# A fused attention and gMLP kernel on one core: the scheduler's landing times of loads and transposes are padded, its transfer durations replaced, and all due times drawn anew

## The chip, the core and the metric

The kernel runs on one core of one Trainium2 chip. The metric is the device time of one launch in microseconds (us), the median of several runs of the same program. In the core, TensorE (PE) multiplies matrices and takes its stationary operand through a weight load (PEld). VectorE (DVE), ScalarE (ACT) and GpSimd (POOL) work on rows of up to 128 partitions, and SyncE (SP) issues all the kernel's transfers (DMAs). Each engine executes its own instruction list strictly in order and waits on semaphores for the others. SBUF is the on-chip memory, PSUM the small memory into which PE writes.

## The reference

Inputs are q, k, v of shape (4, 8, 1152, 64), which is 4 batches of 8 heads, and the weights of a gated MLP. Everything is float32.

```
q_pool = q.reshape(B, H, S // 2, 2, D).mean(axis=3)          # 576 pooled rows per head
scores = (q_pool @ k.T) / sqrt(D)                            # 576 x 1152
attn   = exp(scores - max) / (sum + 1e-9)
x      = (attn @ v), heads side by side                      # (4, 576, 512)

h    = gelu(x @ w_in)                                        # 512 -> 1024
u, v = h[..., :512], h[..., 512:]
v    = layernorm(v) * g_ln
v_s  = w_sg @ v + b_sg                                       # mixes the 576 positions
out  = x + (u * v_s) @ w_out
```

## The kernel before

**Units of work.** The 32 heads are taken as 16 pairs p (four pairs make a batch). In a pair, each head's 1152 keys are nine blocks j of 128 keys. A unit (`attend`, `main`, `unit_of`) is one block of one head against 512 pooled query rows. The last 64 query rows of a head are gathered into two tail units. A unit has two score matmuls (L463), the exponential on ACT (L471), a split of the result into two float16 halves (ACT L477, then a subtraction L482 on DVE or POOL), and twelve small matmuls that weigh the values into the accumulator `avp` (L491). Pairs 0 and 2 skip the split and weigh in float32 (L498).

**Preparing a pair** (`load`, `prepare`, `maxima`, `values`). SP loads k (tile `kr`, L239), q (`qr` and `qe`, L242 and L245) and v (`vr`, L249, or `va` directly, L253, for pairs 0 and 2). There is one buffer of each raw tile, so a pair's k can only be loaded when the pair before it has finished with `kr`. ACT sums the squares of k (L285), PE spreads the sum over the partitions (one small matmul, L288), and DVE makes a scale from it (L270 to L295). ACT and DVE then write k in two float16 halves (L318, L321), and SP transposes them (L325). The same is done for q (POOL L313 and L315, ACT L331, DVE L335, transposed at L339) and for v (L285, L288, L361, L364). PE then computes all the scores once only for their row maxima (L388), and DVE reduces them (L394, collected at L418). POOL splits the maxima (L424 to L426), and a third transpose (L429) puts them beside q so that the second score matmul subtracts them.

**The gMLP of a batch** (`project`, `gmlp`) comes after its 8 heads. PE transposes x (L565) and multiplies by w_in (L641). The layer norm has its statistics on DVE (L666), its normalisation on DVE (L680 writes a float32 row block, L684 its float16 half) and the other half on POOL (L688). Then PE mixes the positions (L641 with `wsg`, L741) and multiplies by w_out (L641 with `wout_h` and `wout_l`, twelve matmuls per output block). The matmuls of one batch's gMLP are spread among the attention units of the next. Only the last batch's stand alone at the end. The weights themselves are split into two parts early in the kernel (`weights`, with L857, L858, L864, L867 on DVE and L870, L876 on POOL).

**Order.** Nothing is issued in the order of the program text. Every piece of work is added to a list with its engine, an assumed duration, what it reads and writes, and a due time. `Schedule.run` then plays the list against a simple model of the engines while the program is built. Each engine takes, of its pieces that could start earliest, the one with the smallest due time. What comes out is only the order on each engine's list. On the chip the semaphores decide when anything starts. For a transfer the model says:

```
dma = max(t + 1.35, dma) + dur        # the queue is busy for dur
free[e] = max(t + issue, dma - AHEAD) # when SP can issue again
end = dma + 0.9                       # when the data count as landed
```

The due times come from tables of numbers (`D_LK` for the load of k, `D_X` for the maxima, and so on, with a column each for pairs 0, 1, 2, 3, 4 to 11, and 12 to 15), read by `lead`.

At the start PE also runs up to 40 matmuls on constant data (L804) that produce nothing the kernel needs.

Of the kernel before, what the change touches and what calls it, by code (L numbers as in the profile page):

```python
# [21 lines left out]
class Schedule:  # L22
# [11 lines left out]

    def add(self, eng, dur, fn, r=(), w=(), due=0.0, acq=None, rel=(), tab=None, start=0.0, port=False, issue=0.5):
        n = len(self.ops)
        deps = set()
        for t in r:
            if t in self.writer:
                deps.add(self.writer[t])  # L40
            self.readers.setdefault(t, []).append(n)
        for t in w:
            if t in self.writer:
                deps.add(self.writer[t])
            deps.update(self.readers.get(t, ()))
# [3 lines left out]
        self.ops.append((eng, dur, fn, deps, round(due + 0.00137, 2), acq, rel, tab, start, port, issue))  # L49

# [4 lines left out]
    def run(self, look):  # L55
        ops = self.ops
# [15 lines left out]
        for _ in ops:  # L72
            for e in engines:
# [3 lines left out]
                for i in can[e]:  # L77
# [3 lines left out]
                    if ops[i][9]:  # L81
                        t = max(t, port)
# [6 lines left out]
            t, i, e = min((t, i, e) for e, (t, i) in choice.items())  # L89
            _, dur, fn, _, _, acq, rel, tb, _, shared, issue = ops[i]  # L90
            can[e].remove(i)
# [38 lines left out]
def attention_gmlp_kernel(  # L130
# [102 lines left out]
    def load(p):  # L233
# [68 lines left out]
    def prepare(p):  # L302
# [5 lines left out]
        for h in range(2):  # L308
# [38 lines left out]
            add("SP", 0.41, k_copy, r=[f"k1{c}{h}"], w=[f"k2{c}{h}"], due=t + lead("KC", p) + h * HS[p > 0])  # L347
            add("DVE", 0.46, q_lo, port=True, r=[f"qs{h}", sct, f"n1{h}"], w=[f"n2q{h}"], due=t + lead("QL", p) + h * HS[p > 0])
# [21 lines left out]
    def maxima(p):  # L370
# [34 lines left out]
        for r in range(9):  # L405
# [6 lines left out]
            if r in (4, 8):  # L412
# [19 lines left out]
                add("POOL", 0.76, split, r=[], w=[f"nm{h}", f"n2m{h}"], due=due - 0.5)  # L432
                add("SP", 0.9, turn, issue=1.25, r=[f"n2q{h}", f"n2m{h}"], w=[f"q2{c}{h}"], due=due - 1)

# [394 lines left out]
    def weights(i):  # L829
# [47 lines left out]

        add("SP", 1.46 * ks, ld, r=["sgdone"], w=rt, due=due - 4)
        add("DVE", 0.68 * ks, s0, port=True, r=rt + ["sgdone"], w=mt + et, due=due)
# [133 lines left out]
KEEP = (0.5, 0.5)  # L1013
D_LK = (-1505.8, -1000.85, -165.08, 526.48, 736.52, 688.03)
D_LQ = (484.61, -1082.79, 1016.76, 1252.2, 668.71, 1.89)
D_LV = (281.6, 307.72, -557.03, 495.8, -509.12, -447.84)
D_SC = (165.08, -128.04, -685.32, -1035.46, -362.92, -1153.53)
D_PL = (-1835.97, -262.1, -273.75, 852.48, 106.54, -40.22)
D_QH = (-1892.34, 165.59, 721.49, 179.72, 662.34, 655.56)
D_KH = (138.62, 145.13, -178.82, -35.67, 780.77, 749.18)  # L1020
D_KC = (-142.4, 635.61, 29.25, -1173.71, -539.16, -997.0)
D_QL = (771.92, -299.43, -364.25, -671.26, 1125.27, 1471.97)
D_VS = (-861.69, -1728.92, 766.42, -696.66, -828.5, -432.59)
D_VH = (-464.47, 768.08, -814.46, -1485.68, 329.36, 378.93)
# [56 lines left out]
```

## Time and profile before

| what | value |
|---|---|
| runs | 680.47, 678.55, 679.84 us (median 679.84) |
| the profiled execution, its own time | 682.78 us |
| its span, first to last instruction | 681.0 us |
| PE busy | 638.4 us (94% of the span) |
| DVE, ACT, POOL busy | 527.8, 523.4, 396.9 us |
| weight loads (PEld) busy | 459.0 us, beside PE |
| mean share of the 16 DMA engines | 43.0% for the kernel's own queue |

The profile is of one execution, 2.94 us longer than the median of the runs shown, and 1.78 us of it lie outside the span. A busy PE is not necessarily a fast one: the clock that was granted to it is given beside it, as a share of full speed (1.00 is 2.4 GHz, 0.50 is 1.2 GHz). An engine's idle time is put down to what ended it.

### The profile page before, as it was taken

To read this page: it belongs to the slowest core of one execution; us is meant where nothing else is said; L and a number is where in the kernel's file an instruction comes from. 1 tells how busy PE (TensorE), PEld (TensorE's weight loads), DVE (VectorE), ACT (ScalarE), POOL (GpSimd) and SP (SyncE) were. 2 spreads that over 40 slices of the span, in tenths; PEclk is the share of its full clock that TensorE was granted. 3 is DMA by queue.
4 is the path that set the end of the run, shared out by engine and by line. 5 is a ranking of instruction groups with operands and counts; after the bars stand their busy time and mean duration, and the time that the engine had idled before them with its cause. 6 is when DMAs were issued, how large, how long until landed. Compare 5 with 4: busy or idle time off the path is not lost. (4 is left out here: it accounts for less than half of the span.)

```text
span 681.0 us, 18291 instructions
## 1 busy us (share of the span) xinstructions
PE 638.4 (94%) x7248; PEld 459.0 (67%) x7250; DVE 527.8 (78%) x1066; ACT 523.4 (77%) x971; POOL 396.9 (58%) x489
## 2 busy tenths in 40 slices
PE   6997979997999899999989999999989999999997
PEld 4476748865677674666667765666767775777955
DVE  4996699797789987889778987799869897633462
ACT  7474897699999677979879879888989897972220
POOL 7252666557465766965343776865555675950072
PEclk9997899999999999999999999999999999999999
DMA  8798554733942206385822216373563301201002
GB/s 233 220 232 154 134 135 123 162 49 79 227 99 53 46 1 155 62 211 100 173 57 57 48 36 150 49 188 72 135 150 60 68 19 21 23 33 39 1 1 69
DMA packets 110133, 66.76 MB, mean 98 GB/s; under 512 B 88480, under 2 KB 92576, under 8 KB 109920
## 3 DMA queue, kind: packets, MB, share of 16 engines
q1 hardware_dynamic: 110048, 65.61, 43.0%
q8 instruction: 56, 0.92, 0.6%
q14 instruction: 29, 0.24, 0.1%
HBM read 36.23 MB, written 4.72 MB: 60 GB/s over the span
## 5 line engine op out<-in xcount | busy, mean ns | idle before, releaser
L482 POOL TENSOR_TENSOR f<-e,f 128x512 f16<-128x512 f32 (+2 forms) x182 | 194.5, 1075 | 113.4 <-ACT f L477 87.5
L463 PE MATMUL s<-q,k 128*128 128x512 f16 (+1 forms) x1152 | 229.8, 289 | 11.0 <-ACT e L471 4.3
L394 DVE TENSOR_REDUCE mp<-px 128x1 f32<-128x512 f32 (+2 forms) x315 | 197.0, 662 | 24.8 <-PE px L388 23.8
L491 PEld LDWEIGHTS <-f 128*128 128x128 f16 x3780 | 151.9, 97 | 55.6 <-issue 9.3
L491 PE MATMUL avp<-va,f 128*128 128x65 f16 x3780 | 166.6, 193 | 0.8 <-POOL f L482 0.2
L471 ACT ACTIVATE e<-s 128x512 f32<-128x512 f32 (+2 forms) x226 | 124.2, 552 | 29.2 <-PE s L463 16.0
L388 PE MATMUL px<-k,q 128*128 128x512 f16 (+1 forms) x448 | 116.9, 328 | 6.2 <-DVE mp L394 3.2
L463 PEld LDWEIGHTS <-k 128*128 128x128 f16 x1152 | 80.2, 100 | 60.4 <-issue 31.3
L477 ACT ACTIVATE f<-e 128x512 f16<-128x512 f32 (+2 forms) x182 | 106.4, 586 | 12.8 <-PE avp L491 8.8
L482 DVE TENSOR_TENSOR f<-s,f 128x512 f16<-128x512 f32 x126 | 86.1, 683 | 34.8 <-ACT f L477 28.6
L477 ACT ACTIVATE f<-s 128x512 f16<-128x512 f32 x126 | 76.9, 610 | 5.7 <-PE avp L491 2.3
L471 ACT ACTIVATE s<-s 128x512 f32<-128x512 f32 x126 | 76.3, 606 | 2.9 <-PE s L463 2.5
L388 PEld LDWEIGHTS <-q 128*128 128x128 f16 x480 | 41.1, 98 | 29.8 <-issue 8.3
L498 PEld LDWEIGHTS avp<-va,e 128*128 128x128 f32 x360 | 50.0, 205 | 4.5 <-issue 0.9
L498 PE MATMUL avp<-va,e 128*128 128x65 f32 x360 | 49.1, 283 | 0.0
L313 POOL TENSOR_TENSOR qs<-qr 128x256 f32<-128x256 f32 x32 | 25.6, 800 | 31.5 <-DVE n L335 20.7
L641 PE MATMUL px<-wout_h,xg 128*128 128x512 f32 x112 | 42.7, 423 | 0.0
L641 PE MATMUL px<-wsg,vz 128*128 128x512 f16 x168 | 41.2, 379 | 0.7 <-POOL vz L688 0.6
L537 POOL TENSOR_TENSOR x<-a,dn 128x320 f32<-128x320 f32 x32 | 24.8, 775 | 28.0 <-DVE dn L534 21.1
L641 PE MATMUL px<-win_h,xg 128*128 128x512 f32 x104 | 38.8, 423 | 0.0
L641 PEld LDWEIGHTS <-vz 128*128 128x128 f16 x224 | 20.4, 98 | 23.6 <-POOL vz L688 1.7
L641 PE MATMUL pm<-xg,win_h 128*128 128x288 f32 x152 | 34.0, 317 | 0.4 <-DVE u L613 0.4
(160 smaller groups left out, 1083.5 us busy)
## 6 DMA issues: line engine op xcount, KB each, us to landing
kr<-in_k_dram SPq DMA_DIRECT2D x16, 576.0 KB, 4.7
qr<-in_q_dram SPq DMA_DIRECT2D x16, 512.0 KB, 4.0
vr<-in_v_dram SPq DMA_DIRECT2D x14, 576.0 KB, 5.2
k<-k SPq DMA_DIRECT2D x32, 144.0 KB, 2.8
x<-in_moe_w_in_dram SPq DMA_DIRECT2D x8, 512.0 KB, 5.4
out_dram<-t SPq DMA_DIRECT2D x16, 256.0 KB, 2.1
x<-in_moe_w_out_dram SPq DMA_DIRECT2D x8, 256.0 KB, 3.0
u<-in_moe_w_sg_dram SPq DMA_DIRECT2D x1, 1152.0 KB, 7.2
```

The costliest lines, as they stand in the source:

```text
L313: nc.gpsimd.tensor_tensor(out=qs[:, 6 * h:6 * h + 4, :], in0=qr[:, h, :, 0, :], in1=qr[:, h, :, 1, :], op=ALU.add)
L388: nc.tensor.matmul(out=bank(x)[:, w * i:w * i + w], lhsT=q1[c][:, o, :], rhs=k1[c][:, h, j0:j0 + nj, :].rearrange("p j k -> p (j k)"), sta ...
L394: nc.vector.tensor_reduce(out=mp[c][:, r0:r0 + len(group), g], in_=src, axis=AX.X, op=ALU.max)
L463: nc.tensor.matmul(out=buf(("s", u))[:, col:col + w], lhsT=kk[c][:, hh, j, :], rhs=qq[:, o:o + w], start=(i == 0 and m == 0), stop=(i == 1 ...
L471: nc.scalar.activation(out=s if kept else buf(("e", u))[:, 0:n], in_=s, func=AF.Exp, scale=SCALE * 2.0**-ASH)
L477: nc.scalar.activation(out=buf(("f", u))[:, 0, 0:n], in_=exponentials(), func=AF.Copy)
L482: eng.tensor_tensor(out=f[:, 1, 0:n], in0=exponentials(), in1=f[:, 0, 0:n], op=ALU.subtract)
L491: nc.tensor.matmul(out=avp[:, o:o + m], lhsT=w[:, col:col + 128], rhs=vv, start=(j == 0 and k == 0 and not tail and x == 0), stop=(j == KJ ...
L498: nc.tensor.matmul(out=avp[:, o:o + D + 1], lhsT=e[:, col:col + 128], rhs=vw[c][:, KJ * hh + j, :], start=(j == 0 and k == 0 and not tail) ...
L537: nc.gpsimd.tensor_tensor(out=xbuf[b % 2][:, :, col], in0=a[:, :, 0:D], in1=d.rearrange("p (i o) -> p i o", o=1).to_broadcast([128, 5, D]) ...
L641: nc.tensor.matmul(out=bank(m)[:, 0:cols], lhsT=l, rhs=r, start=(k + j == 0), stop=(k + j == n - 1))
```

## The change

Every transfer gets a fourth number, `late`, which is added to the time at which the model counts its data as landed. For the loads of k, q and v of pairs 1 to 15 and for the loads of w_in and w_out it is 1.5, and for the transposes of q and k, the copy of k (L328) and the transpose of the maxima, from pair 1 on, 0.5. The assumed durations of transfers are replaced: 1.9 becomes 1.7 for k and v, 3.3 becomes 2.4 for the wide v, 0.9 becomes 0.7 for the transposes of q and of the maxima, and 1.42 becomes 1.1 for the transpose of k. The tables of due times and the start limits are replaced as well. No instruction, tile, buffer count or assignment of work to an engine changes: `KEEP`, `NBUF`, `TAILS`, `F32P` and `WARM` are as before.

```diff
-    def add(self, eng, dur, fn, r=(), w=(), due=0.0, acq=None, rel=(), tab=None, start=0.0, port=False, issue=0.5):
+    def add(self, eng, dur, fn, r=(), w=(), due=0.0, acq=None, rel=(), tab=None, start=0.0, port=False, issue=0.5, late=0.0):
...
             if e == "SP":
                 dma = max(t + 1.35, dma) + dur
                 free[e] = max(t + issue, dma - AHEAD)
-                end = dma + 0.9
+                end = dma + 0.9 + late
...
-        add("SP", 1.9, lk, w=["kr"], due=t + lead("LK", p), start=R_K if p == 1 else 0.0)
+        add("SP", 1.7, lk, late=LATE[0] * (p > 0), w=["kr"], due=t + lead("LK", p), start=R_K if p == 1 else 0.0)
...
-            add("SP", 3.3, lv_wide, w=parts, due=t + lead("LV", p) if p else -11.0, start=R_V[p] if p < 2 else 0.0)
+            add("SP", 2.4, lv_wide, late=LATE[0] * (p > 0), w=parts, due=t + lead("LV", p) if p else -11.0, start=R_V[p] if p < 2 else 0.0)
...
-            add("SP", 0.9, q_turn, issue=1.25, r=[f"n1{h}"], w=[f"q1{c}{h}"], due=t + lead("QH", p) + h * HS[p > 0])
+            add("SP", 0.7, q_turn, late=LATE[1] * (p > 0), issue=1.25, r=[f"n1{h}"], w=[f"q1{c}{h}"], due=t + lead("QH", p) + h * HS[p > 0])
...
-            add("SP", 1.42, k_turn, issue=1.3, r=[f"kh{h}", f"kl{h}"], w=[f"k1{c}{h}"], due=t + lead("KH", p) + h * HS[p > 0])
+            add("SP", 1.1, k_turn, late=LATE[1] * (p > 0), issue=1.3, r=[f"kh{h}", f"kl{h}"], w=[f"k1{c}{h}"], due=t + lead("KH", p) + h * HS[p > 0])
...
-D_LK = (-1505.8, -1000.85, -165.08, 526.48, 736.52, 688.03)
+D_LK = (-2128.44, -1144.14, -343.27, 737.94, 161.12, 600.61)
...
-R_K, R_Q, R_V, R_S, R_Z = 23.29, 22.68, (7.06, 17.98), 0.0, 0.0
+R_K, R_Q, R_V, R_S, R_Z = 23.25, 21.8, (12.45, 9.4), 0.0, 0.0
...
+LATE = (1.5, 0.5, 0.5)
```

What the new numbers do to the order is seen only in the instruction lists. Three places stand here, each before and now. (Names end in a buffer's number; `xN` counts repeats.)

**ACT, pair 10 to pair 11.** The first row before, L318, writes the second half of pair 10's k and is the last reader of `kr` on ACT. The last row, L285, sums the squares of pair 11's k, for which the next load of `kr` must have landed. The rows between are exponentials (L471), splits (L477) and gelu copies for the gMLP (L599):

```order
L318 ACTIVATE kn<-kr,sc_105 128x9x64 x2
L471 ACTIVATE s_134<-s_134 128x512
L599 ACTIVATE vz<-px_138 128x512
L471 ACTIVATE e_124<-s_136 128x512
L599 ACTIVATE vz<-px_137 128x512
L471 ACTIVATE s_136<-s_136 128x512
L477 ACTIVATE f_131<-e_126 128x512
L477 ACTIVATE f_128<-s_135 128x512
L285 ACTIVATE kn,am_100<-kr 128x1152
```

Now the last L318 stands two rows ahead of these, with one more full exponential (L471) between:

```order
L471 ACTIVATE s_136<-s_136 128x512
L477 ACTIVATE f_129<-e_125 128x512
L471 ACTIVATE e_124<-s_135 128x512
L477 ACTIVATE f_130<-s_136 128x512
L471 ACTIVATE s_134<-s_134 128x512
L477 ACTIVATE f_131<-e_124 128x512
L477 ACTIVATE f_128<-s_134 128x512
L471 ACTIVATE e_126<-s_135 128x256
L477 ACTIVATE f_129<-e_126 128x256
L599 ACTIVATE vz<-pm_140 128x512
L471 ACTIVATE e_127<-s_136 128x512
L285 ACTIVATE kn,am_100<-kr 128x1152
```

Seven instructions stood between the two uses of `kr`; now there are twelve, two of them of half width.

**DVE, the layer norm of batch 0.** Before, two reductions of maxima (L394, which free the PSUM tiles that PE's next score matmuls need) stand behind normalisation instructions (L680, L684) and two steps of splitting a weight piece (L864, L867):

```order
L613 COPY u<-pm_140 128x288
L684 CAST vz<-t_132 128x512
L680 TENSOR_SCALAR t_133<-vz,mv,rs 128x512
L864 SCALAR_TENSOR_TENSOR x_89<-x_89 128x256
L684 CAST vz<-t_133 128x512
L867 SCALAR_TENSOR_TENSOR x_89<-x_89 128x256
L394 TENSOR_REDUCE mp_81<-px_137 128x1
L394 TENSOR_REDUCE mp_81<-px_138 128x1
L482 TENSOR_TENSOR f_128<-s_135,f_128 128x512
```

The same normalisation now, from the same L864 on:

```order
L864 SCALAR_TENSOR_TENSOR x_89<-x_89 128x256
L680 TENSOR_SCALAR t_132<-vz,mv,rs 128x512
L680 TENSOR_SCALAR t_133<-vz,mv,rs 128x512
L613 COPY u<-px_138 128x288
L684 CAST vz<-t_132 128x512
L684 CAST vz<-t_133 128x512
L482 TENSOR_TENSOR f_130<-s_134,f_130 128x512
L613 COPY u<-px_137 128x288
L867 SCALAR_TENSOR_TENSOR x_89<-x_89 128x256
L680 TENSOR_SCALAR t_132<-vz,mv,rs 128x512
L613 COPY u<-px_139 128x288
L684 CAST vz<-t_132 128x512
```

No reduction of maxima stands in the normalisation any more; copies of the u projection (L613, each behind twelve L641 matmuls of 128x288) do, and one subtraction of the attention (L482). From the first row shown to the normalisation's last instruction (L691, 23 rows on) 17 DVE instructions read and write SBUF alone (L680, L684, L690, L691, and L857 to L867 of two weight pieces); two L482 of the attention stand behind them, 19 rows after the one shown here.

**PE, behind the last attention unit.** The twelve L491 of the last unit of pair 15 end in the first row. Before, eight matmuls of batch 2's last product (L641 with `wout_h`, `wout_l`) and the transposes of x of batch 3 (L565) come next:

```order
L491 MATMUL avp<-va_87,f_131 128x65
L641 MATMUL px_137<-wout_h,xg 128x512
L641 MATMUL px_137<-wout_l,xg 128x512
L641 MATMUL px_137<-wout_h,xg 128x512
L641 MATMUL px_137<-wout_l,xg 128x512
L565 MATMUL pm_140<-ident,x_89 128x128 x4
L641 MATMUL px_137<-wout_h,xg 128x512
L641 MATMUL px_137<-wout_l,xg 128x512
L641 MATMUL px_137<-wout_h,xg 128x512
L641 MATMUL px_137<-wout_l,xg 128x512
L565 MATMUL px_139<-ident,x_89 128x128 x4
```

Now the same product goes on for longer (the pattern is kept up over `px_138`, `px_139` and four more of `px_137`):

```order
L491 MATMUL avp<-va_87,f_131 128x65
L641 MATMUL px_137<-wout_h,xg 128x512
L641 MATMUL px_137<-wout_l,xg 128x512
L641 MATMUL px_137<-wout_h,xg 128x512 x2
L641 MATMUL px_137<-wout_l,xg 128x512
L641 MATMUL px_137<-wout_h,xg 128x512 x2
L641 MATMUL px_137<-wout_l,xg 128x512
L641 MATMUL px_137<-wout_h,xg 128x512 x2
L641 MATMUL px_137<-wout_l,xg 128x512
L641 MATMUL px_137<-wout_h,xg 128x512
L641 MATMUL px_138<-wout_h,xg 128x512
L641 MATMUL px_138<-wout_l,xg 128x512
```

In all 44 of these matmuls stand there now, where 8 stood: 36 have moved from the attention of batch 3 to behind it.

## Rows read from the trace of the kernel before

**Rows 1.** The page, busy time by engine, share of the span, and instructions.

```profile
PE 638.4 (94%) x7248; PEld 459.0 (67%) x7250; DVE 527.8 (78%) x1066; ACT 523.4 (77%) x971; POOL 396.9 (58%) x489
```

**Rows 2.** Five stretches (us from the start): busy time by engine, granted clock, DMA.

```profile
core 0: us, PE busy (x) PEld busy (x) DVE busy (x) ACT busy (x) POOL busy (x), PEclk, DMA share, GB/s
17.00:30.20 13.20, 12.51 (x58) 5.02 (x58) 13.10 (x27) 4.75 (x8) 2.61 (x7) 1.00 0.77 199
57.60:72.80 15.20, 11.32 (x55) 9.42 (x55) 5.13 (x12) 7.53 (x14) 5.02 (x5) 0.55 0.71 173
236.00:244.00 8.00, 8.00 (x82) 6.46 (x81) 7.16 (x14) 4.11 (x8) 2.92 (x2) 0.79 0.20 51
374.00:612.00 238.00, 232.40 (x3054) 164.73 (x3051) 189.01 (x376) 207.59 (x388) 158.62 (x189) 1.00 0.35 75
616.00:676.00 60.00, 58.77 (x352) 44.69 (x351) 26.48 (x52) 14.69 (x19) 19.12 (x17) 1.00 0.06 21
```

**Rows 3.** PE's waits: waiting line and its releaser, us in total, times, longest.

```profile
PE px L288 <- ACT kn L285: 12.3, 4, 6.1
...
PE px L288 <- ACT va L285: 3.9, 4, 1.5
...
PE s L463 <- DMA q<-n: 2.2, 2, 1.2
PE px L388 <- DMA q<-n: 2.1, 2, 1.8
```

**Rows 4.** The page, DMA issues: count, size of one, median us to landing.

```profile
kr<-in_k_dram SPq DMA_DIRECT2D x16, 576.0 KB, 4.7
...
vr<-in_v_dram SPq DMA_DIRECT2D x14, 576.0 KB, 5.2
```

**Rows 5.** Timeline of the start: start, duration, instruction, [idle before].

```profile
9.32 3.59 SPq L325 DMA_TRANSPOSE k<-kn  x1
13.95 2.52 SPq L339 DMA_TRANSPOSE q<-n  x2
...
17.62 0.38 PE L388 MATMUL px<-k,q 128*128 128x512 f16 x1
...
18.59 0.62 SPq L249 DMA_DIRECT2D vr<-in_v_dram  x1
...
26.09 0.15 DVE L295 TENSOR_SCALAR sc<-sc 128x1 f32<-128x1 f32 x1
```

**Rows 6.** Timeline, ACT and PE, squares and spread of pair 3's k.

```profile
60.32 1.16 ACT L285 ACTIVATE kn<-kr 128x1152 bf16<-128x1152 f32 x1 [4.20 <-DMA kr<-in_k_dram]
...
61.62 0.16 PE L288 MATMUL px<-am,unit_b 128*128 128x1 bf16 x1 [3.88 <-ACT kn L285]
```

**Rows 7.** Timeline, the same two instructions for pair 11.

```profile
344.86 1.16 ACT L285 ACTIVATE kn<-kr 128x1152 bf16<-128x1152 f32 x1 [2.82 <-DMA kr<-in_k_dram]
...
346.17 0.16 PE L288 MATMUL px<-am,unit_b 128*128 128x1 bf16 x1 [1.99 <-ACT kn L285]
```

**Rows 8.** Timeline, DVE in batch 0's normalisation, and PE's wait behind it.

```profile
230.63 1.38 DVE L864 SCALAR_TENSOR_TENSOR x<-x 128x256 f32<-128x256 uint32 x1
...
231.94 1.38 DVE L684 CAST vz<-t 128x512 f16<-128x512 f32 x1
...
233.23 1.37 DVE L867 SCALAR_TENSOR_TENSOR x<-x 128x256 int32<-128x256 int32 x1
...
235.25 0.38 PE L388 MATMUL px<-k,q 128*128 128x512 f16 x1 [2.55 <-DVE mp L394]
```

**Rows 9.** One line, L867: duration in ns, shortest, median, longest; where.

```profile
L867 DVE SCALAR_TENSOR_TENSOR x<-x x8: 409/414/1369, 127.1 to 265.3; 128x256 int32<-128x256 int32 x8
```

**Rows 10.** The page, groups of instructions: count, busy us, mean ns, idle before.

```profile
L498 PE MATMUL avp<-va,e 128*128 128x65 f32 x360 | 49.1, 283 | 0.0
...
L641 PE MATMUL pm<-xg,win_h 128*128 128x288 f32 x152 | 34.0, 317 | 0.4 <-DVE u L613 0.4
```

**Rows 11.** The chain that ended last, in the final gMLP: start, duration, instruction.

```profile
671.59 2.80 PE pm L641 x12
```

More of the change, by code (lines that the diff above doesn't have):

```diff
@@ L48, in add @@
         port = port or (eng == "POOL" and dur > 0)
-        self.ops.append((eng, dur, fn, deps, round(due + 0.00137, 2), acq, rel, tab, start, port, issue))
+        self.ops.append((eng, dur, fn, deps, round(due + 0.00137, 2), acq, rel, tab, start, port, issue, late))
     def buf(self, h):
@@ L89, in run @@
             t, i, e = min((t, i, e) for e, (t, i) in choice.items())
-            _, dur, fn, _, _, acq, rel, tb, _, shared, issue = ops[i]
+            _, dur, fn, _, _, acq, rel, tb, _, shared, issue, late = ops[i]
             can[e].remove(i)
@@ L256, in ones @@
             nc.vector.memset(vw[p % 2][:, :, D:D + 1] if wide else va[p % 2][:, :, 2 * D:2 * D + 1], 1.0)
-        add("SP", 1.9, lk, w=["kr"], due=t + lead("LK", p), start=R_K if p == 1 else 0.0)
-        add("SP", 1.9, lq, w=["qr"], issue=1.6, due=t + lead("LQ", p), start=R_Q if p == 1 else 0.0)
+        add("SP", 1.7, lk, late=LATE[0] * (p > 0), w=["kr"], due=t + lead("LK", p), start=R_K if p == 1 else 0.0)
+        add("SP", 1.9, lq, late=LATE[0] * (p > 0), w=["qr"], issue=1.6, due=t + lead("LQ", p), start=R_Q if p == 1 else 0.0)
         parts = [f"v{a}{p % 2}{h}" for a in "hl" for h in range(2)]
@@ L263, in load @@
         if p in F32P:
-            add("SP", 3.3, lv_wide, w=parts, due=t + lead("LV", p) if p else -11.0, start=R_V[p] if p < 2 else 0.0)
+            add("SP", 2.4, lv_wide, late=LATE[0] * (p > 0), w=parts, due=t + lead("LV", p) if p else -11.0, start=R_V[p] if p < 2 else 0.0)
         else:
-            add("SP", 1.9, lv, w=["vr"], due=t + lead("LV", p) if p else -11.0, start=R_V[p] if p < 2 else 0.0)
+            add("SP", 1.7, lv, late=LATE[0] * (p > 0), w=["vr"], due=t + lead("LV", p) if p else -11.0, start=R_V[p] if p < 2 else 0.0)
     def root(m, ps):
@@ L432, in maxima @@
                 add("POOL", 0.76, split, r=[], w=[f"nm{h}", f"n2m{h}"], due=due - 0.5)
-                add("SP", 0.9, turn, issue=1.25, r=[f"n2q{h}", f"n2m{h}"], w=[f"q2{c}{h}"], due=due - 1)
+                add("SP", 0.7, turn, late=LATE[2] * (p > 0), issue=1.25, r=[f"n2q{h}", f"n2m{h}"], w=[f"q2{c}{h}"], due=due - 1)
     def attend(g):
@@ L876, in s5 @@
             nc.gpsimd.tensor_tensor(out=l, in0=mf, in1=f32(h), op=ALU.subtract)
-        add("SP", 1.46 * ks, ld, r=["sgdone"], w=rt, due=due - 4)
+        add("SP", 1.46 * ks, ld, late=LATE[0], r=["sgdone"], w=rt, due=due - 4)
         add("DVE", 0.68 * ks, s0, port=True, r=rt + ["sgdone"], w=mt + et, due=due)
@@ new lines @@
+D_LQ = (780.32, -799.05, 643.7, 2022.5, 1268.52, 128.54)
+D_LV = (575.7, 1660.52, -260.44, 992.28, -1248.58, 0.23)
+D_SC = (716.08, 217.21, -553.63, -229.25, -966.46, -1410.78)
+D_PL = (-1513.49, -653.83, -577.72, 902.54, 858.37, 119.89)
+D_QH = (-2290.56, -362.42, 563.28, -24.24, 497.02, 361.59)
+D_KH = (1154.18, 329.08, -108.78, -103.35, 598.66, 897.03)
+D_KC = (-153.79, 128.58, -522.62, -863.05, -143.26, -1460.64)
+D_QL = (579.66, 243.96, -1171.5, 70.32, 639.06, 1689.64)
+D_VS = (-592.25, -1860.97, 1164.2, -456.51, -989.73, -1333.83)
@@ L1033 @@
+D_VH = (-152.75, 797.52, -1246.43, -1579.03, 558.61, 571.61)
+D_X = (-121.96, -98.04, 432.22, 118.51, 5.24, 6.6)
+D_XS = (-6.881, 6.301, 6.862, 0.445, 0.557, 0.497)
+D_E1 = (115.89, 162.58, -1214.92, 57.95, 21.68, -142.44)
+D_E2 = (-141.47, -115.38, -193.81, -68.68, -361.8, -567.52)
+D_AV = (35.3, -604.93, 116.32, -75.06, -665.01, 3.28)
+D_M0, D_MS, D_LN = -4.07, 117.2, 32.21
+WI0, WID, WO0, WOD = 306.96, 0.368, 304.02, -6.734
+SG0, SGD, SGS = -606.84, 1063.6, 35.96
 NBUF = (4, 4, 2)
 LOOK = 0
-HS = (6.427, 22.055)
+HS = (2.892, 18.549)
```

20 lines of the change are left out of this document (1 added, 19 removed).

## Prediction

> **What bounds the kernel now.** I read the page first. PE is busy 638.4 us of the span, 94%; ACT and DVE follow at 77% and 78% [rows 1]. The span can only shrink where PE waits, or where PE is busy at a low clock. The change touches no instruction, so its whole effect must lie in these two. The span is 681.0 us, so PE is idle for 42.6 us.
>
> The table of PE's waits says who is waited for [rows 3]. Waits that end in a landed transfer are what the change aims its numbers at: the squares of k (12.3 us in four waits, the longest of which, 6.1, lies at the very start of the program, before any order matters), the squares of v (3.9 in four), and transposed q or maxima (2.2 and 2.1, two each). Without the first 6.1 that is 14.4 us.
>
> Then I read the stretches by clock [rows 2]. PE runs at 0.55 of full speed over 57.6 to 72.8 and at 0.79 over 236 to 244, each time right behind a long wait of PE: 3.88 us for pair 3's k [rows 6], and 2.55 us for a reduction of maxima [rows 8]. A stall here costs its own length and then the lower clock. 11.32 us of busy PE at 0.55 hold 6.2 us of work at full clock, so that stall's clock costs about 5.1 us; 8.00 us at 0.79 cost 1.7.
>
> In the attention of the last batches (374 to 612) PE is busy 232.40 of 238 us, ACT 207.59 [rows 2]. PE is the bound there, with ACT next at 87%.
>
> **The change part by part.** The model counted a load as landed 1.35 + 1.9 + 0.9 = 4.15 us after its issue; it now says 1.35 + 1.7 + 0.9 + 1.5 = 5.45. The profile's medians are 4.7 for k and 5.2 for v [rows 4]. So the model was about 0.5 to 1 us too early and is now 0.3 to 0.8 too late. For a transpose of q the model goes from 3.15 to 3.45. A later landing in the model costs nothing on the chip by itself; it lets the scheduler put other work in front of the instruction that waits. What the order really does decides.
>
> *Pair 11's k.* ACT waited 2.82 us for the load and PE 1.99 behind it [rows 7]. Between the last use of the old `kr` on ACT and these squares there were seven instructions, and now there are twelve, two of them of half width. ACT's 388 instructions of 374 to 612 take 207.59 / 388 = 0.54 us each on average [rows 2], which makes 3.8 us then and 6.4 now. So 2.6 us of the wait of 2.82 are filled, and PE's own wait was shorter than ACT's. On PE, too, more attention units stand between the spreads of pairs 10 and 11: 11.2 by a count in its list, instead of 5.3. I take **-2.0**; bounds 0, if the load is issued later, and -2.0.
>
> *Pair 3's k.* ACT was idle for 4.20 us until this load landed, and PE for 3.88 [rows 6]. On PE there are 8.3 units between the spreads of pairs 2 and 3, where there were 8.0. So next to nothing was put in front of this wait. 0.3 of a unit, whose twelve L498 matmuls alone are 12 x 49.1 / 360 = 1.6 us [rows 10], is about **-0.6**; bounds 0 and -9.0 (3.88 and the 5.1 of clock).
>
> *DVE in the normalisation of batch 0.* Three instructions took 1.38, 1.38 and 1.37 us, and two reductions stood behind them; PE waited 2.55 for the PSUM tiles [rows 8], and the clock fell. In the new order there is no reduction of maxima in the whole normalisation. The wait and its clock go: **-4.2** (2.55 + 1.7); bounds 0, if something else waits there, and -4.2.
>
> *Start.* On SP, v of pair 1 is now loaded ahead of the first transpose of k, and the two wide loads of pair 0's v stand behind it, ahead of the q transposes. Before, the q transposes were issued at 13.95, and the first maximum's matmul ran at 17.62 [rows 5]; what delays these transposes delays pair 0. The first k transpose ended its issue at 9.32 + 3.59 = 12.91, so two issues of about 0.62 each (that of the other v load) end at 14.15: 0.2 late. But the two loads also carry 576 KB ahead of the transposes, and at the 199 GB/s of that stretch [rows 2] that is 3.0 us. In return four small DVE instructions that make pair 1's scale of v, each as long as L295's 0.15 [rows 5], leave a stretch in which DVE is full (13.10 of 13.20 [rows 2]): -0.6. Bounds -0.4 and +3.0. The loads are issued while the 16 engines are busy 0.77 of the time, so they are neither free nor alone; I take **+1.1**, a little under the middle.
>
> *The other landing waits.* What is left is 0.35 for k, 3.9 for v and 4.3 for q: 8.5 us [rows 3]. A margin removes at most what it adds: 1.3 us of each of four v waits (3.7 of 3.9, as only the longest exceeds it), and 0.3 of each of four transpose waits (1.2). That is 4.9. Pair 3 shows that a margin need not reach the order, so I take half, **-2.5**; bounds 0 and -8.5.
>
> *PE behind the last unit.* 36 matmuls of batch 2's last product move behind the attention. Each is 2.80 / 12 = 0.233 us [rows 11], so 8.4 us of PE work moves. PE is 98% busy in the attention that gives them up and 98% in the final gMLP that takes them (58.77 of 60 [rows 2]); what is added there is taken away here, and I put the move at 0. The cover is PE's being the bound in the attention; if it were not, the price is the full 8.4 (below).
>
> Sum: 1.1 - 4.2 - 2.0 - 0.6 - 2.5 = **-8.2 us**. Against the profiled execution of 682.78 that is 674.6. That execution was 2.94 us above the median of the runs, 679.84, and the same step taken from the median gives **671.6 us**, 1.2% less. The likeliest case's own range is 666 to 677.5.
>
> **The rivals.**
> *The stall at pair 3 goes as well.* The due times of pairs 2 and 3 are all new, so the load may be issued earlier on the chip than before. Then 3.88 - 0.6 and the clock's 5.1 go too: 671.6 - 8.4 = 663.2. Against it: the units in front of the spread are as many as before.
>
> *DVE's normalisation becomes the wait.* Between the first L864 and the end of the normalisation stand 17 DVE instructions in SBUF alone, with POOL at work beside them. One such instruction took 0.41 at its shortest and median and 1.37 at its longest [rows 9], and three in a row were long before [rows 8]. PE's cover in the run is five groups of twelve u matmuls, 60 x 34.0 / 152 = 13.4 us [rows 10]; 17 short ones are 7.0 us and 17 long ones 23.4. From 7 long ones on the run outlasts the cover. At 12 it is 5.2 us over, with 1.7 of clock, 678.5; at 17 10.0 over, 683.3.
> The Trainium skill (SBUF — State Buffer, Who interferes with whom) says that a DVE instruction with two SBUF inputs contends with a GpSimd instruction that reads SBUF, and that the one that issues second blocks until the first is finished; a reduction never does. The rows of 1.37 against 0.41 agree. By that rule taken strictly, with POOL at work throughout, this change packs the instructions that block into one run, and the time is that of 17 long ones; by the rows' median the run is covered.
>
> *ACT sets the attention's length (the other side).* If PE's waits in the attention only take up what ACT's chain of exponential and split leaves over, filling them wins nothing, and the 36 matmuls taken out of the attention leave holes in place of work, while the 8.4 us are added at the end: 679.84 + 1.1 + 8.4 = 689.3. It decides where PE's idle time over the last batch's attention grows by as much as is taken out. For it: ACT is at 87% there, and its instructions hang on PE's in a ring of few buffers. Against it: PE at 98%.
>
> *The waits only move.* A stall filled at pair 11 comes back at the next pair, since one buffer of `kr` ties each load to the pair before: 679.8.
>
> **How the numbers follow.** Chances: forecast 0.50, pair 3 too 0.14, normalisation 0.13, ACT 0.15, moved waits 0.08. 0.3%, or 2.0 us, is about what a measurement of this kernel tells from no change: faster is under 677.8, slower over 681.9. The forecast counts 0.48 faster and 0.02 same; pair 3 is faster; the normalisation 0.05, 0.06 and 0.02; moved waits 0.06 same and 0.02 slower; ACT slower. That is 0.67, 0.14 and 0.19. The range from 661 to 684 leaves out ACT and the best ends of the pair 3 case.
>
> **What would show it.** Right: no wait of 2 us for pair 11's spread and none behind a reduction near 235, with a clock of 1.00 there; the wait at pair 3 still at 3 to 4 us with half clock behind it; the first maximum's matmul at about 18.5; PE as full as before up to the last unit, which ends some 16 us earlier, and a final stretch 8.4 us longer. Wrong: PE busy well under 97% over the last batch's attention, a run of L684 and L864 at 1.4 us with PE idle beside it, or the first second score late by 3 us.

## The result and the profile after

| | median, us | runs |
|---|---|---|
| before | 679.33 | 678.55 to 680.47, four runs on the same chip |
| changed | 664.24 | 664.03 to 664.97, four runs |

The ratio is 0.978 (95% interval 0.976 to 0.980): 15.1 us less, faster. The profiled execution of the changed kernel is an ordinary one (664.26 us, span 662.4). That of before (682.78, span 681.0) lay 3.4 above its median, so the two traces differ by 18.6 us where the medians differ by 15.1. What follows is an account of the traces.

The page of the changed kernel, its first part; it answers to [rows 1].

```profile
PE 631.8 (95%) x7250; PEld 453.8 (68%) x7250; DVE 530.0 (80%) x1066; ACT 524.3 (79%) x971; POOL 393.9 (59%) x489
```

PE is idle for 662.4 - 631.8 = 30.6 us, 12.0 less than before, and busy for 6.6 us less with the same matmuls. The larger part of that is clock: the mean granted over the span was 0.984 and is 0.991, which over some 635 us of busy time is 4.4 us; the rest I can't place. 12.0 and 6.6 are the 18.6. Who PE waits for, in us in total, times and longest, answers to [rows 3]:

```profile
PE px L288 <- ACT kn L285: 6.7, 2, 6.0
PE s L463 <- DVE f L482: 3.9, 7, 1.0
PE s L463 <- ACT e L471: 3.6, 7, 1.6
PE avp L491 <- DVE f L482: 2.2, 3, 1.4
PE px L388 <- DMA q<-n: 1.8, 1, 1.8
PE px L952 <- DVE wsg L967: 1.2, 2, 1.0
```

The wait for v is gone from the list, and of the waits for k little but the one at the program's start is left. Without that one the waits for landed transfers were 6.2 + 3.9 + 2.2 + 2.1 = 14.4 us, and are 0.7 + 1.8 = 2.5. That is 11.9 of the 12.0 us of idle time; the other waits only changed places among themselves (PE's 3.6 us for reductions, L394, fell to 0.3, and 2.2 us for subtractions ahead of L491 are new).

The stretches, with busy times, granted clock and DMA as in [rows 2]. The first has the same bounds as there, the third holds the normalisation of batch 0, the last two are the attention and the final gMLP at their new places:

```profile
57.60:72.80 15.20, 15.18 (x165) 11.95 (x163) 14.21 (x29) 14.99 (x30) 10.15 (x12) 1.00 0.91 208
80.00:88.00 8.00, 6.42 (x85) 4.38 (x84) 7.86 (x23) 7.22 (x14) 4.42 (x8) 0.79 0.42 91
...
222.00:248.00 26.00, 25.26 (x257) 17.77 (x255) 24.37 (x40) 21.23 (x36) 17.56 (x16) 1.00 0.32 69
350.00:588.00 238.00, 235.17 (x3124) 168.36 (x3123) 197.77 (x385) 216.44 (x399) 159.34 (x189) 1.00 0.35 74
589.00:649.00 60.00, 58.77 (x353) 44.82 (x353) 25.93 (x51) 14.27 (x18) 18.71 (x17) 1.00 0.06 20
```

Over 57.6 to 72.8 PE is now busy for 15.18 us at full clock, where it was busy for 11.32 at 0.55: 165 matmul records stand there instead of 55. About half of the gain comes from here, as is shown below. The normalisation runs at 1.00, where the clock had been 0.79. The dip at 80 to 88 (0.79), behind a wait of 1.41 us for a subtraction, has its like before: 0.79 over 96 to 104, behind a wait of 2.00 us for a subtraction. New in this trace are dips at 17 to 30.2 (0.87, where [rows 2] has 1.00) and at 156 to 166 (0.83, behind a wait of 1.55 us). The timelines of ACT and PE at pair 3, to be read against [rows 6]:

```profile
58.41 1.15 ACT L285 ACTIVATE kn<-kr 128x1152 bf16<-128x1152 f32 x1
...
60.38 0.17 PE L288 MATMUL px<-am,unit_b 128*128 128x1 bf16 x1
```

Neither row has a bracket: neither engine waits. PE comes to the spread at 60.38, where it had come at 61.62 - 3.88 = 57.74; the squares are done 1.9 us earlier than before.

How that came about is seen from the spread of pair 2's k on. Here is the stretch from that spread to the one of pair 3's k, and the issue of pair 3's k load. Before:

```profile
45.03:61.62 16.59, 12.71 (x104) 10.25 (x104) 12.23 (x28) 9.07 (x17) 4.07 (x7) 0.92 1.03 219
```

```profile
54.30 0.54 SPq L239 DMA_DIRECT2D kr<-in_k_dram  x1
```

After:

```profile
46.78:60.38 13.60, 13.60 (x117) 10.96 (x117) 13.50 (x31) 10.40 (x19) 4.78 (x7) 1.00 1.12 254
```

```profile
52.50 0.57 SPq L239 DMA_DIRECT2D kr<-in_k_dram  x1
```

PE has only 0.9 us more work in front of pair 3's spread (12.71 and 13.60). The load moved more: it was issued 9.27 us after pair 2's spread and is now issued 5.72 after it, and the squares start 11.63 us after that spread instead of 15.29.

What stall and clock cost together is read from the first copy of an accumulator (ACT L530) to the second, before first and after second:

```profile
50.81:75.81 25.00, 21.12 (x143) 17.77 (x141) 12.12 (x28) 12.61 (x25) 7.87 (x11) 0.73 0.84 167
```

```profile
51.33:66.88 15.55, 15.55 (x138) 13.49 (x137) 14.54 (x31) 12.14 (x24) 5.88 (x9) 1.00 0.98 200
```

That is 9.4 us less: the 3.88 of the stall, and 5.6 of PE's busy time at about as many matmul records. In two other traces with the order of before (the runs with 30 matmuls fewer and with short pieces, below) this stretch took 23.3 and 24.3 us, so 0.7 to 1.7 of the 9.4 belong to the one execution profiled here.

The end, the last copy of an accumulator (ACT L530) of each kernel, before first and after second:

```profile
616.02 0.45 ACT L530 ACTIVATE a<-avp 128x325 f32<-128x325 f32 x1 [6.37 <-PE avp L491]
```

```profile
589.06 0.45 ACT L530 ACTIVATE a<-avp 128x325 f32<-128x325 f32 x1
```

The attention ends 27.0 us earlier, and from there to the end of the span it takes 73.3 us instead of 65.0: 8.3 of the 27.0 are given to the 36 matmuls that moved.

### The profile page after: what moved, and what is told of

The parts are those of the page before. It is cut to its first block, busy times and chain, and to the rows that moved or that the text cites. A ratio compares the mean times of both kernels' runs of the same rounds, so it can differ in the third digit from the quotient of the medians.

```text
span 662.4 us, 18269 instructions
## 1 busy us (share of the span) xinstructions
PE 631.8 (95%) x7250; PEld 453.8 (68%) x7250; DVE 530.0 (80%) x1066; ACT 524.3 (79%) x971; POOL 393.9 (59%) x489
## 4 chain that ended last, share of the span: by engine, by line
PE 64%; DVE 15%; ACT 10%; DMA 4%; issue 3%; POOL 2%; SPq 0%; ACTq 0%; POOLq 0%; DVEq 0%
PE s L463 15%; PE px L641 13%; PE avp L491 12%; PE pm L641 8%; PE px L388 8%; PE avp L498 6%; DVE mp L394 5%; ACT f L477 3%; DVE f L482 2%; ACT e L471 2%; DVE va L364 2%; DMA q<-n 2%; DMA qr<-in_q_dram 1%; ACT s L471 1%; POOL f L482 1%
## 5 line engine op out<-in xcount | busy, mean ns | idle before, releaser
L482 POOL TENSOR_TENSOR f<-e,f 128x512 f16<-128x512 f32 (+2 forms) x182 | 196.2, 1086 | 103.5 <-ACT f L477 80.0
L394 DVE TENSOR_REDUCE mp<-px 128x1 f32<-128x512 f32 (+2 forms) x318 | 199.8, 662 | 23.3 <-PE px L388 22.5
L491 PEld LDWEIGHTS <-f 128*128 128x128 f16 x3780 | 150.1, 98 | 58.4 <-issue 10.2
L491 PE MATMUL avp<-va,f 128*128 128x65 f16 x3780 | 169.4, 194 | 3.5 <-DVE f L482 2.2
L471 ACT ACTIVATE e<-s 128x512 f32<-128x512 f32 (+2 forms) x226 | 124.6, 554 | 31.9 <-PE s L463 20.4
L388 PE MATMUL px<-k,q 128*128 128x512 f16 (+1 forms) x451 | 117.9, 328 | 2.8 <-DMA q<-n 1.8
L477 ACT ACTIVATE f<-e 128x512 f16<-128x512 f32 (+2 forms) x182 | 106.9, 590 | 4.5 <-PE avp L491 1.2
L482 DVE TENSOR_TENSOR f<-s,f 128x512 f16<-128x512 f32 x126 | 86.0, 683 | 29.8 <-ACT f L477 24.8
L471 ACT ACTIVATE s<-s 128x512 f32<-128x512 f32 x126 | 76.8, 610 | 10.5 <-PE s L463 10.4
L477 ACT ACTIVATE f<-s 128x512 f16<-128x512 f32 x126 | 77.3, 614 | 4.0 <-PE avp L491 1.2
L388 PEld LDWEIGHTS <-q 128*128 128x128 f16 x480 | 41.8, 99 | 27.8 <-issue 4.8
L498 PEld LDWEIGHTS avp<-va,e 128*128 128x128 f32 x360 | 46.3, 191 | 4.2 <-issue 0.8
L498 PE MATMUL avp<-va,e 128*128 128x65 f32 x360 | 45.6, 270 | 0.0
L641 PE MATMUL px<-wsg,vz 128*128 128x512 f16 x168 | 43.3, 379 | 0.6 <-POOL vz L688 0.6
L641 PEld LDWEIGHTS <-vz 128*128 128x128 f16 x224 | 20.7, 98 | 23.5 <-issue 1.1
L641 PE MATMUL px<-wout_h,xg 128*128 128x512 f32 x96 | 34.6, 414 | 0.0
L641 PE MATMUL pm<-win_h,xg 128*128 128x512 f32 x88 | 33.6, 428 | 0.0
L321 DVE SCALAR_TENSOR_TENSOR kn<-kr,sc,kn 128x576 f16<-128x576 f32 x32 | 31.5, 996 | 2.1 <-ACT kn L318 1.9
```

Source lines behind the costliest of these rows:

```text
L321: nc.vector.scalar_tensor_tensor(out=kn[:, h, :, 1, :], in0=kr[:, h], scalar=s[:, 0:1], in1=kn[:, h, :, 0, :], op0=ALU.mult, op1=ALU.subtract)
L388: nc.tensor.matmul(out=bank(x)[:, w * i:w * i + w], lhsT=q1[c][:, o, :], rhs=k1[c][:, h, j0:j0 + nj, :].rearrange("p j k -> p (j k)"), sta ...
L394: nc.vector.tensor_reduce(out=mp[c][:, r0:r0 + len(group), g], in_=src, axis=AX.X, op=ALU.max)
L471: nc.scalar.activation(out=s if kept else buf(("e", u))[:, 0:n], in_=s, func=AF.Exp, scale=SCALE * 2.0**-ASH)
L477: nc.scalar.activation(out=buf(("f", u))[:, 0, 0:n], in_=exponentials(), func=AF.Copy)
L482: eng.tensor_tensor(out=f[:, 1, 0:n], in0=exponentials(), in1=f[:, 0, 0:n], op=ALU.subtract)
```

## The experiments

All times are medians; ratios are to the kernel before on the same chip, with the 95% interval. The kernel before took 679.8 to 680.1 us beside them and 679.33 beside the changed kernel, so a difference to the changed kernel's 664.24 is good to about 1 us.

### The margins alone, the due times alone

**Margins at zero.**

```diff
-LATE = (1.5, 0.5, 0.5)
+LATE = (0.0, 0.0, 0.0)
```

> The changed kernel with all three margins at 0, its new due times, limits and durations kept. If the margins are what puts work in front of the landing waits, these come back: PE's waits for landed transfers (squares of k and v without the first, transposed q) rise from 2.4 us to 8 or more, and the time is 672 to 680 us. Rival, the new due times alone carry the gain: within 3 us of the changed kernel's 664.2, with these waits under 4 us.

Measured: 693.71 us, ratio 1.022 (1.016 to 1.027). Slower than the kernel before, and beyond what either theory gave. PE's waits in this kernel:

```profile
PE px L288 <- ACT kn L285: 10.4, 4, 6.7
...
PE px L388 <- DMA k<-kn: 3.5, 3, 1.5
PE px L388 <- DVE mp L394: 3.4, 6, 1.4
...
PE s L463 <- DMA q<-n: 2.8, 2, 1.5
PE pm L388 <- DVE mp L394: 2.8, 1, 2.8
PE px L288 <- ACT va L285: 1.1, 2, 0.7
...
PE pm L288 <- ACT kn L285: 0.7, 1, 0.7
```

The landing waits are back at 3.7 + 3.5 + 2.8 + 1.1 + 0.7 = 11.8 us, as the first theory said, and 6.2 us for reductions came on top. The new due times by themselves carry nothing.

**Margins and durations with the old due times.**

```diff
-D_LK = (-2128.44, -1144.14, -343.27, 737.94, 161.12, 600.61)
+D_LK = (-1505.8, -1000.85, -165.08, 526.48, 736.52, 688.03)
...
-R_K, R_Q, R_V, R_S, R_Z = 23.25, 21.8, (12.45, 9.4), 0.0, 0.0
+R_K, R_Q, R_V, R_S, R_Z = 23.29, 22.68, (7.06, 17.98), 0.0, 0.0
...
 LATE = (1.5, 0.5, 0.5)
```

> The changed kernel's margins and durations with the due times and start limits of the kernel before. If the margins do the work by themselves, the landing waits fall from 14.4 us (without the first) to under 7 and the time is 672 us or less. Rival, margins and due times only work together, since every due time was drawn for the order that the old landing times gave: 679 us or more, with other waits in the place of those that go.

Measured: 686.03 us, ratio 1.009 (1.006 to 1.012). The landing waits fell to 5.1 us (0.6 for k, 1.5 for v, 3.0 for q), so the margins do what they are for in an order that nobody fitted to them; but PE's waits for reductions rose from 3.6 to 7.5 us and those for exponentials (L471) from 4.3 to 5.7, and in all PE is idle for 43.2 us, where it was 42.6. The rival was right: neither half is worth anything alone.

**The load margin at 1.4.**

```diff
-LATE = (1.5, 0.5, 0.5)
+LATE = (1.4, 0.5, 0.5)
```

> The changed kernel with the margin of the loads at 1.4 instead of 1.5, due times kept. If the size of the margin is what works, 0.1 us of it changes next to nothing: within 2 us of 664.2. Rival, the due times were drawn for the one order that 1.5 gives, and any other landing time deals a new one that nothing was fitted to: 670 us or more.

Measured: 677.43 us, ratio 0.997 (0.994 to 0.999). A tenth of a microsecond in the model costs 13 us: the rival. PE's landing waits are up again, from 2.5 to 6.3 us. The size of the margin isn't what makes 664.

**The old durations.**

```diff
-        add("SP", 1.7, lk, late=LATE[0] * (p > 0), w=["kr"], ...)
+        add("SP", 1.9, lk, late=LATE[0] * (p > 0), w=["kr"], ...)
...
-            add("SP", 1.1, k_turn, late=LATE[1] * (p > 0), ...)
+            add("SP", 1.42, k_turn, late=LATE[1] * (p > 0), ...)
```

> The changed kernel with the transfer durations of the kernel before (1.9, 3.3, 0.9, 1.42), margins and due times kept. The model's landings come 0.2 to 0.9 later still, so if late landings alone are what covers the waits, the landing waits stay under 4 us and the time within 3 us of 664.2. Rival, as with the smaller margin, a new order that nothing was fitted to: 670 us or more, with waits of other kinds.

Measured: 678.66 us, ratio 0.999 (0.996 to 1.001). PE's waits in this kernel:

```profile
PE px L388 <- DVE mp L394: 8.3, 18, 1.1
PE px L288 <- ACT kn L285: 6.7, 2, 6.4
PE s L463 <- ACT e L471: 5.0, 12, 0.8
PE avp L491 <- DVE f L482: 4.3, 10, 0.8
PE avp L491 <- POOL f L482: 3.3, 7, 1.2
PE s L463 <- DMA q<-n: 1.1, 2, 0.7
...
PE px L388 <- DMA k<-kn: 0.8, 1, 0.8
```

This is the clearest of the five. The landing waits are 0.3 + 1.1 + 0.8 = 2.2 us, as few as in the changed kernel, and still the time is that of before: many short waits for DVE and POOL (8.3, 4.3, 3.3) stand in their place. Covering the landings isn't enough. Nor is it the clock, which was 0.998 over this span and 0.991 over the changed kernel's: PE is idle for 41.3 us here, and for 30.6 there.

**The transposes' margins at 0.4.**

```diff
-LATE = (1.5, 0.5, 0.5)
+LATE = (1.5, 0.4, 0.4)
```

> The changed kernel with the margins of the transposes at 0.4 instead of 0.5. The order of the transfers stays but for two swaps late in the program, and that of POOL nearly. Both theories expect little here, since the early order is the same: the margin's size 664 to 666, the fitted order 664 to 668, by what the few moved instructions of pairs 12 to 15 cost.

Measured: 665.38 us, ratio 0.979 (0.973 to 0.985). As both theories had it, so it separates nothing; it shows that a change of the margin that leaves nearly the whole order alone leaves the time alone too.

### The stall at pair 3

The four kernels here have every instruction in the place that it has in the kernel they come from; only pair 3's k load differs.

**Before, with a short load** (one block of nine).

```diff
-nc.sync.dma_start(out=kr.rearrange(...), in_=k[b, hs].rearrange(...))
+nc.sync.dma_start(out=kr[:, :, 0], in_=k[b, hs].rearrange("h (p j) d -> p h j d", j=KJ)[:, :, 0]) if p == 3 else nc.sync.dma_start(...)
```

> The kernel before with every instruction in its place, but of pair 3's k only one block of nine is loaded (the rest is pair 2's, so pair 3's result is another). If the late load was the cause of stall and clock, PE's wait of 3.88 us shrinks to under 2, the half clock behind it goes, and the time falls by 6 to 9 us to 670 to 673. Rival, another late event stands right behind it (a q transpose landed at 60.8 as well): PE waits for that instead, and the time falls by less than 2.

Measured: 678.60 us, ratio 0.999 (0.997 to 1.001). A ninth of the data lands hardly earlier. ACT's squares in its timeline:

```profile
59.55 1.16 ACT L285 ACTIVATE kn<-kr 128x1152 bf16<-128x1152 f32 x1 [2.84 <-DMA kr<-in_k_dram]
```

SP had issued the load at 53.51, so these 64 KB took some 6.0 us, as long as the 576 KB of before (54.30 to 60.32, [rows 6]). At this place it is not the size of a load that sets when it lands. The time is the rival's, but not for its reason: the squares still stand for the load, and PE for the squares, 2.52 us.

**Before, without the load.**

```diff
+            p == 3 or nc.sync.dma_start(...)
```

> The kernel before with every other instruction in its place, but pair 3's k isn't loaded at all (pair 2's is used again, so pair 3's result is another). If this load's landing was what PE stood for, the stall of 3.9 us and its half clock (about 5) go: 671 to 674 us, and the granted clock over 57 to 73 is 1.00. Rival, a q transpose that lands at the same time takes its place: at most 3 us gained, with the clock still at 0.8 or less there.

Measured: 678.04 us, ratio 0.997 (0.995 to 1.000). The squares and PE's spread:

```profile
58.23 1.16 ACT L285 ACTIVATE kn<-kr 128x1152 bf16<-128x1152 f32 x1 [2.02 <-DMA k<-kn]
```

```profile
59.53 0.16 PE L288 MATMUL px<-am,unit_b 128*128 128x1 bf16 x1 [1.69 <-ACT kn L285]
```

The rival was right on the time and the clock; what takes the load's place isn't a q transpose, though. The squares also overwrite `kn`, so they stand for pair 2's k transposes, which read it, and these land only 2.1 us ahead of the load. PE still waits 1.69 us, and the clock over 57 to 73 is still 0.79. In the order of before, two landings were late at the same place, and to take one away wins 1.9 us (0.2 to 3.7).

**Changed, with pieces of 256 bytes.**

```diff
+[nc.sync.dma_start(out=kr[:, h], in_=k[b, 2 * hp + h].rearrange("(j p) d -> p j d", j=KJ)) for h in range(2)] if p == 3 else nc.sync.dma_start(...)
```

> The changed kernel with every instruction in its place, but pair 3's k is loaded in pieces of 256 bytes (its keys in another order, so pair 3's result is another). The load lands later by some x us, 1 to 4. If a stall at this place costs its own length and then the clock, PE waits about x at pair 3's spread, the granted clock behind it is 0.5 for some 10 us, and the time is x + 4 to 6 above 664.2: 669 to 674. Rival, the clock's fall there has another cause: only x or less is lost, 664 to 668, and the clock stays at 1.00.

Measured: 664.78 us, ratio 0.978 (0.976 to 0.981). ACT's squares:

```profile
59.73 1.16 ACT L285 ACTIVATE kn<-kr 128x1152 bf16<-128x1152 f32 x1 [0.71 <-DMA kr<-in_k_dram]
```

They start 1.3 us later than in the changed kernel's trace. Of that 0.5 was there before the load (the first accumulator's copy is at 51.84, not at 51.33), so the pieces cost 0.8. PE's spread, at 61.04, still has no wait, but the squares end only at 60.99. This says nothing of the clock, since there was no stall; it shows that the cover of the new order is thin here. In the changed kernel the squares end at 59.66 and the spread runs at 60.38, 0.7 us later.

**Changed, with pieces of 128 bytes in four transfers.**

```diff
+[nc.sync.dma_start(out=kr[:, h, :, 32 * c:32 * c + 32], in_=k[b, 2 * hp + h].rearrange("(j p) d -> p j d", j=KJ)[:, :, 32 - 32 * c:64 - 32 * c]) for h in range(2) for c in range(2)] if p == 3 else nc.sync.dma_start(...)
```

> The changed kernel with every instruction in its place, but pair 3's k is loaded in pieces of 128 bytes by four transfers (keys and columns in another order, so pair 3's result is another). 256 bytes made it 1.3 us later, and PE did not wait. If the cover that PE has there is thin (2 us or less) and a stall also costs the clock, PE waits 2 us or more at pair 3's spread, the clock falls to 0.5 to 0.8 behind it, and the time is 669 to 674. Rival, the new order covers even a load that is 4 us late: 666 or less, clock 1.00.

Measured: 670.48 us, ratio 0.985 (0.982 to 0.989), 6.2 above the changed kernel; the four runs lie between 667.31 and 671.82. PE's spread, and the stretch of twelve microseconds around and behind it (columns as in [rows 2]):

```profile
60.80 0.16 PE L288 MATMUL px<-am,unit_b 128*128 128x1 bf16 x1 [1.43 <-ACT kn L285]
```

```profile
60.00:72.00 12.00, 10.87 (x74) 9.31 (x74) 8.15 (x16) 9.35 (x18) 5.81 (x6) 0.72 0.94 223
```

The stall is back, 1.43 us long, and the half clock behind it: 10.87 us busy at 0.72 are 3.0 lost. With the stall that is 4.5 us. The profiled execution, 669.18 us, lies 4.9 above that of the changed kernel, so 0.4 is left over in the traces (the four issues also hold SP for 4.74 us); the 6.2 between the medians I can't place in full. The first theory holds for the clock and the time; the stall is shorter than the 2 us that it asked for, a third as long as that of before.

### The matmuls behind the last unit

In both kernels 30 of the 36 moved matmuls are left out, ten of twelve in each of three output blocks:

```diff
-nc.tensor.matmul(out=bank(m)[:, 0:cols], ...)
+(m[1:] in ((2, 'o', 1), (2, 'o', 2), (2, 'o', 3)) and 0 < k + j < n - 1) or nc.tensor.matmul(out=bank(m)[:, 0:cols], ...)
```

> The kernel before, with 30 of the 36 matmuls left out (ten of twelve in three output blocks of batch 2's last product, which is then another result); they stand in the attention of batch 3. If PE is the bound there, the time falls by 30 x 0.233 = 7.0 us. Rival, ACT sets the attention's length: less than 2 us.

Measured: 675.74 us, ratio 0.993 (0.991 to 0.996): by the ratio 4.5 us less (3.1 to 6.0). From the 24th copy of an accumulator to the last, the traces with these matmuls (before, short load, no load, short pieces) take 136.0 to 136.6 us, of which PE is idle for 1.8 to 2.4, and this one 131.1 with 3.4 idle.

> The changed kernel with the same 30 matmuls left out; they stand behind the last attention unit. They are on the path there if nothing else delays the final gMLP: 7.0 us less, 657.2. If both this and the same cut in the kernel before give 7 us, the move was free; if only this one does, the move cost 8.4 us and other gains were larger by as much.

Measured: 656.41 us, 7.8 below the changed kernel. That looks like the whole price of the 30 matmuls, but the traces, whose spans differ by 7.7, place it otherwise. From the last copy of an accumulator to the end of the span it takes 68.3 us instead of 73.3, 5.0 less; the other 2.7 lie ahead of that copy, where both programs have the same instructions. Without the matmuls PE waits behind the last unit for the x of batch 3:

```profile
593.57 0.66 PE L565 MATMUL px<-ident,x 128*128 128x128 f32 x4 [1.64 <-DVE t L769]
```

So the matmuls were worth some 5 of their 7.0 us in the attention of before (3.1 to 6.0 by the medians), and some 5 at the end, where they cover 1.64 us of a wait. PE was the bound in the attention for most of the time and not all. Since the end did grow by 8.3 us with all 36, the move cost some 3 us in the order of before: 8.3 less 36/30 of 4.5 (1 to 5, by the interval of the 4.5).

### The long DVE instructions

The kernel before, with L864 and L867 of the w_out pieces on a quarter of the columns:

```diff
-nc.vector.scalar_tensor_tensor(out=mf, in0=lw, scalar=2.0**-32, in1=m, ...)
+nc.vector.scalar_tensor_tensor(out=mf[:, :, 0:256 if ks > 0.9 else 32], in0=lw[:, :, 0:256 if ks > 0.9 else 32], scalar=2.0**-32, in1=m[:, :, 0:256 if ks > 0.9 else 32], ...)
```

> The kernel before with every instruction in its place, but the two DVE steps L864 and L867 of the w_out pieces work on a quarter of the columns (so w_out is another). If their 1.38 us is their own work, they fall to about 0.2 and the wait of 2.55 us behind them, with its clock, goes: 3 to 4 us less than before, 676. Rival, they stand for something outside them, POOL's instruction beside them: they stay near 1 us at a quarter of the work, PE's wait stays over 1.5 us, and the time is within 2 us of before.

Measured: 679.87 us, ratio 0.999 (0.997 to 1.001). DVE in the normalisation, then POOL over the same time:

```profile
230.34 1.18 DVE L864 SCALAR_TENSOR_TENSOR x<-x 128x64 f32<-128x64 uint32 x1
231.44 1.40 DVE L684 CAST vz<-t 128x512 f16<-128x512 f32 x1
232.75 1.17 DVE L867 SCALAR_TENSOR_TENSOR x<-x 128x64 int32<-128x64 int32 x1
```

```profile
230.03 1.40 POOL L482 TENSOR_TENSOR f<-e,f 128x512 f16<-128x512 f32 x1 [0.35 <-ACT f L477]
231.39 1.15 POOL L688 TENSOR_TENSOR vz<-t,vz 128x512 f16<-128x512 f32 x1
232.53 1.31 POOL L482 TENSOR_TENSOR f<-e,f 128x512 f16<-128x512 f32 x1
```

A quarter of the work takes 1.18 and 1.17 us, where 1.38 and 1.37 stood [rows 8]; the shortest of this width in the same trace took 0.18 (L864) and 0.21 (L867). L864 ends at 231.52, L482 on POOL at 231.43; L867 at 233.92, the next L482 at 233.84. The DVE instruction ends when POOL's does: it stands for POOL. This agrees with the Trainium skill (SBUF — State Buffer, Who interferes with whom), by which, of a DVE instruction with two SBUF inputs and a GpSimd instruction that reads SBUF, the second to issue blocks until the first is finished. The rival was right, and PE still waits 2.18 us behind these. Making the instructions smaller doesn't remove the wait at this place; in the new order no reduction stands behind them, and PE doesn't wait there.

## Why the prediction was right, and where it wasn't

The direction was right and the range held the time; the size came out at nearly twice the forecast. The likeliest case's own range, 666 to 677.5, did not hold it; the full range did, because the rival at pair 3 was counted in. By the steps of the sum:

*Pair 3, -0.6: the step that failed.* "So next to nothing was put in front of this wait" was right: the work that PE has there grew by 0.9 us. (The price of a unit was too high: it has four L498, eight records of the trace, which take 1.0 us, and not twelve.) What failed is that the sum took this work as all that could close the wait and left the load where it was. SP issues it at 52.50 instead of 54.30, and counted from pair 2's spread 3.55 us earlier; with the 0.9 of work that closes 3.88. This is the condition of the rival in which the stall at pair 3 goes as well, which I gave 0.14. With the stall and its clock the stretch takes 9.4 us less, where the rival had 3.88 and 5.1. The rival's time, 663.2, against 664.24, is in part chance, since the terms below were off on both sides and make up for each other. Delaying the load again (670.48) brings stall and clock back together. The short and the missing load of before won 0.9 us (not clear of noise) and 1.9 us: in the old order the load alone, as my sum had taken it, was not the cause, but with it the k transposes of pair 2 right beside it. SP issues the last of these earlier too (51.10 for 51.42, and it is done with it 1.8 us sooner); which of the two landings the new order needed more wasn't tried.

*The other landing waits, -2.5: mis-sized.* The halving leaned on pair 3, and the cap didn't hold: the waits for q and the maxima fell from 4.3 us to 1.8, twice the 1.2 that the margins were taken to remove, and those for v are gone. Of 8.5 us 2.5 are left, so this term was -6.

*Pair 11, -2.0, and the normalisation of batch 0, -4.2: right.* Pair 11's spread has no wait, nor has any L388 behind a reduction near the normalisation, and the clock there is 1.00. (The 1.7 of clock in the -4.2 is that of one execution: in the trace of before with 30 matmuls fewer the same wait, 2.55 us, was followed by full clock.) The rival of a DVE run that outlasts its cover had its mechanism right (the quarter-width run shows it) and didn't come about: the 17 instructions took 11.4 us together, inside the 13.4 of cover, and PE is busy for 25.26 of 26 us there.

*Start, +1.1: right at its place, half as much behind it.* The first maximum's matmul runs at 18.84 instead of 17.62, 1.2 late, but the first accumulator's copy only 0.5 late.

*The moved matmuls, 0: mis-sized, by about +3.* The final stretch did grow by 8.3 us; what the attention of before gives up without them is less. The 3 us are inferred from the order of before; in the changed trace no row shows them, and PE's idle time in the attention of the last batches fell from 5.6 to 2.8 us of 238. The rival in which ACT sets the attention's length holds for a part of it, and not for the sign.

The terms as measured, 0.5 - 9.4 - 6 - 2.0 - 4.2 + 3, are -18.1, against -18.6 between the traces. This is closer than the terms are known: the +3 is inferred, and the new dips at 17 to 30.2 and 156 to 166 and the 2.2 us of subtractions are in the traces and not in this sum.

"A stall here costs its own length and then the lower clock" holds for the two stalls it was read from, and not for every one. In the same trace the 1.99 us of pair 11 [rows 7] were followed by full clock:

```profile
346.20:360.00 13.80, 13.80 (x176) 9.68 (x176) 12.15 (x25) 11.23 (x23) 8.39 (x11) 1.00 0.19 37
```

The wait of 1.41 us ahead of the changed kernel's dip at 80 to 88 stands in the traces with pieces of 256 and of 128 bytes and with 30 matmuls fewer too, 1.41 to 1.42 us long, and there the clock stays at 1.00 for the eight us behind it; in the trace with the transposes' margins at 0.4 (1.40 us) it is 0.79 again. What decides between the two, the runs don't show.

One thing the prediction didn't ask at all. It took the three parts of the change for one, and they are: the margins cover the landings in every order built with them (2.2 to 6.3 us left in five orders, against 14.4 and 11.8 without), but 664 us belongs to the one order that these due times give with just these landings. Why the neighbours at 677 to 686 lose elsewhere was read from their waits only; which of their orders' places costs what stays open.

## What to carry to other kernels

Where a scheduler's model decides the order, a landing time and the due times are one parameter set: judge a margin only with due times drawn for it, and expect a tenth of a microsecond to deal another order. When work is counted in front of a wait, look up too when the transfer is issued, both counted from the same point (here pair 2's spread): a wait also closes from the side of the load. Ask what else the waiting instruction stands for (here the tile it overwrites) before a load is blamed. A PE wait of even 1.5 us can cost the clock behind it as well: here from nothing (1.99 us at pair 11) to twice its own length (1.43 us, with 3.0 behind it).

## What the runs showed of the hardware

The twelve us around and behind a PE wait of 1.43 us ran at a mean 0.72 of full clock, 3.0 us of loss; the 15 us that hold the wait of 3.88 ran at 0.55. A wait of 1.99 us was followed by 14 us at 1.00, and one and the same wait of 1.40 to 1.42 us by a dip in two traces and by full clock in three. A load of 64 KB let its reader start 6.0 us after its issue where 576 KB did the same. A DVE instruction of 64 columns took 1.18 us beside a POOL instruction and 0.18 to 0.21 at its shortest, and ended within 0.1 us of POOL's.
